# Attention, folded weights and two token-wise layers on one core: TensorE in the source's order through attention, sums of two pairs in four strips

## The chip, the cores and the metric

One NeuronCore of a Trainium2 chip runs the whole program in one launch. The metric is the device time of one execution in microseconds (us); the kernel before takes 824.54 us (median of 3 runs, 823.51 to 825.24). The engines are named as in the profile: PE (TensorE, with its weight loads PEld), ACT (ScalarE), DVE (VectorE), POOL (GpSimd), and SP, which only issues transfers.

## The reference

```
# q, k, v: [4, 12, 448, 64]; w1, w2: [768, 1024]; w3: [1024, 1024]; w_out: [1024, 768]
s = cap * tanh((q @ k.T) / sqrt(64) / cap)           # per batch and head, 448 x 448
attn = exp(s - max(s));  attn /= sum(attn) + 1e-9
x = (attn @ v), heads side by side                   # 1792 tokens x 768
h = ((x @ w1) * (x @ w2)) @ w3;  x = h @ w_out       # first layer
h = x @ w_in;  e = exp(h - max(h))                   # second layer
solu = h * (e / (sum(e) + 1e-9))
ln = (solu - mean) / sqrt(var + 1e-6) * g_ln
out = ln @ w_out2
```

Everything is float32. Weights come as 64-bit values in two 32-bit words.

## The kernel before, in words

**Three stretches.** From 0 to 431 us attention runs, and PE's gaps in it are filled with work that doesn't depend on it. From 431 to 581 us the rest of the first layer's products (`ab`, line 592) runs alone. From 581 us to the end the second layer runs; the change doesn't touch it.

**Attention.** The 48 heads are taken two at a time: 24 pairs, `n` = 0 to 23. A pair's 448 keys are four chunks, `c` = 0 to 3; chunks 0 to 2 hold 128 keys of each head, chunk 3 the last 64 keys of both. `scores(n, c, place_)` (line 226) multiplies keys by queries. For chunks 0 to 2 each head takes 64 rows of the array, so two matmuls (one for each head, line 238) stand in the two row halves; they come in three terms (high and low parts), six matmuls to a tile. Chunk 3 fills the whole array (line 234). A tile of scores lies in one of two places of PSUM, `sc0` and `sc1`, and a place can't be written again before ACT has taken tanh and exp of what is in it (`exps`, lines 246 and 247). `keep` (lines 255 to 261) lets DVE add up a pair's four exp tiles into one tile `s`, of which two buffers exist.

**The visit of the values.** `values(n)` (line 263) takes pair n's exp tiles to the output: first `n` (line 275), the sums over keys, by a matrix of ones 64 columns wide, once for each head; then `o` (lines 276 to 280), the exp tiles times v, four chunks for each of two heads. The heads take the two column halves of the array (64 columns each). These matmuls are plain float32; each leaves two records in the trace, so `n` leaves 4 and `o` 16. ACT copies both results out (lines 284, 285). `inverse` (line 290) gathers the sums of two pairs by two transfers of POOL's queue, takes reciprocals on DVE and stores them.

**Fill.** Beside attention stand: `f` of line 360 (the product of w3 and w_out, 576 matmuls of 256 columns), `f` of line 378 (times w_in, 288 of 512 columns), and the first 404 of the 1152 `ab` matmuls (line 592, 448 columns). `fill(ns)` (line 631) emits them from one list, a given nominal time at a call (109, 216 and 189 ns for one matmul). Their weights are loaded as 64-bit values, put together by three DVE instructions (lines 171 to 173) and split into a high part (ACT, line 177) and a low part (DVE, line 178). `ahead.step()` puts one such weight tile forward; it is called at each chunk that `phases` passes.

**Order.** `phases(g)` (line 665) emits two pairs in three phases: phase 0 has chunks (2g, 0) and (2g, 1), then (2g, 3); phase 1 has (2g, 2), (2g+1, 0), then (2g+1, 3); phase 2 has (2g+1, 1), (2g+1, 2). Phases 0 and 2 also hold a visit of the values, of the pair before. Fill of 6100 ns is emitted at the end of each phase from g = 1 on (line 694). But the order in which PE gets its instructions isn't that of the source: a scheduler at build time sorts them by priorities (`tc.high_priority`, lines 670 to 685) and by what a model of the machine holds for ready; `tc.issue_after` pins some of them behind others. What comes out is one fixed list for each engine. The order of DVE, ACT and the queues is the scheduler's too.

Of the kernel before, what the change touches and what calls it, by code (L numbers as in the profile page):

```python
# [9 lines left out]
F32 = mybir.dt.float32  # L10
# [3 lines left out]
ALU = mybir.AluOpType  # L14
# [4 lines left out]
P = 128  # L19
B, H, S, D = 4, 12, 448, 64  # L20
# [5 lines left out]
HALF = 512  # L26
SUMS = 112
# [2 lines left out]
THREE = ((0, 0), (0, 1), (1, 0))  # L30

NP, NCH = B * NPAIR, 4
FIRST = 4
NV = 2 * NCH
EXPS = 7
FILL = 6100
W3 = 9
WARM = 12
LANDS = 3
PASSES = ((0, 1), (2, 3))  # L40
SQ = 32
# [59 lines left out]
def attention_moe_solu(ctx: ExitStack, tc: tile.TileContext, q, k, v, cap, w12, w3t, wo, win, wout2, g_ln, out):  # L101
# [9 lines left out]
    pe, act, dve, pool, sync = nc.tensor, nc.scalar, nc.vector, nc.gpsimd, nc.sync  # L111
# [5 lines left out]
    r_dr = dram.tile([B, H, S], F32, name="r_dr")  # L117
# [6 lines left out]
    const = ctx.enter_context(tc.tile_pool(name="const", bufs=1))  # L124
    capt = const.tile([P, 1], F32, name="capt")
    qscale = const.tile([P, 1], F32, name="qscale")
    guard = const.tile([P, 1], F32, name="guard")
    neghalf = const.tile([P, 1], F32, name="neghalf")
    gt = const.tile([P, LINE // 4], F32, name="gt")[:, :NF]
    ones = const.tile([P, D], F32, name="ones")  # L130
    edge = ctx.enter_context(tc.tile_pool(name="edge", bufs=1, side="right"))
    edge.tile([P, (LINE - 32) // 4], F32, name="edge")
    conv = ctx.enter_context(tc.tile_pool(name="conv", bufs=1))
# [1 line left out]
    def opened(stack, name, side="left"):  # L135
        cm = tc.tile_pool(name=name, bufs=1, side=side, reuse_waits="tile")
        stack.append(cm)
        return cm.__enter__()

    def close(stack, to=0):  # L140
        while len(stack) > to:
            stack.pop().__exit__(None, None, None)

    right, left = [], []
    at = opened(right, "at", "right")
    ps_cm = tc.tile_pool(name="ps1", bufs=1, space=PSUM)
    ps = ps_cm.__enter__()
# [39 lines left out]
        ahead.add(key, lambda: landing(i, src.bitcast(U32), 2 * n, U32), lambda: convert(i, n), rest, gate, there)  # L187


    landed, ready, parts, outs, xr, stored, inv = {}, {}, {}, {}, {}, set(), [None]  # L190

    def load_pair(n):
        if n == 1:
# [26 lines left out]
    def take_values(n):  # L220
        if n < NP:
            ready[n] = *ready[n], landed.pop(n)

    tiled = [None]

    def scores(n, c, place_):

        qh, ql, kh, kl = ready[n][:4]
        sc = ps.tile([P, 2, HALF], F32, tag=f"sc{place_}", name=f"sc{n}_{c}")
        terms = ((kh, ql), (kl, qh), (kh, qh)) if n else ((kh, qh),)  # L230
        for m, (kk, qq) in enumerate(terms):
            keys = kk[:, c * P:(c + 1) * P]
            if c == 3:
                pe.matmul(sc[:, 0, :S], keys, qq, start=(m == 0), stop=(m == len(terms) - 1))
                continue
            for j in range(2):
                rows = slice(j * D, (j + 1) * D)
                tiled[0] = pe.matmul(sc[:, j, :S], keys[rows], qq[rows, :], start=(m == 0), stop=(m == len(terms) - 1))  # L238
        return sc

    exp_ = {}
# [1 line left out]
    def exps(n, c, sc):  # L243
        w = 2 if c < 3 else 1
        p = at.tile([P, w, S], F32, tag="p" if c < 3 else "pl", bufs=EXPS if c < 3 else 3, name=f"p{n}_{c}")
        act.activation(sc[:, :w, :S], sc[:, :w, :S], AF.Tanh, scale=qscale)  # L246
        exp_[n, c] = act.activation(p, sc[:, :w, :S], AF.Exp, scale=capt)  # L247
        return p

    def keep(n, c, p):  # L250

        parts[n, c] = p
        if c == 1:
            parts[n, "s"] = t = at.tile([P, 2, S], F32, tag="s", bufs=2, name=f"s{n}")
            dve.tensor_tensor(t, parts[n, 0], p, ALU.add)  # L255
            for j in range(2):
                rows = slice(j * D, (j + 1) * D)
                dve.tensor_tensor(t[rows, j], t[rows, j], parts[n, NCH - 1][rows, 0], ALU.add)
        elif c == 2:
            t = parts[n, "s"]  # L260
            dve.tensor_tensor(t, t, p, ALU.add)

    def values(n):

        b, m = divmod(n, NPAIR)
        vs = ready[n][4]
        out, total = (ps.tile([P, HALF], F32, tag="o", bufs=2, name=f"{x}{n}") for x in ("o", "n"))
        seen = [None]

        def product(dst, j, weights, moving, first, last):  # L270
            with tc.issue_after(seen[0].ins) if seen[0] is not None else nullcontext():
                seen[0] = pe.matmul(dst[j * D:(j + 1) * D, :S], weights, moving, start=first, stop=last)  # L272

        for j in range(2):
            product(total, j, ones, parts[n, "s"][:, j], True, True)
        for c in range(NCH - 1):
            for j in range(2):
                product(out, j, vs[:, j * (NCH - 1) + c], parts[n, c][:, j], c == 0, False)
        for j in range(2):
            product(out, j, vs[:, 2 * (NCH - 1) + j], parts[n, NCH - 1][:, 0], False, True)  # L280
        t = at.tile([P, S], F32, tag="x", bufs=2, name=f"x{n}")
        if m % 2 == 0:
            xr[b, m // 2] = at.tile([P, 2, S], F32, tag="xr", bufs=3, name=f"xr{b}_{m // 2}")
        act.copy(xr[b, m // 2][:, m % 2], out[:, :S])
        act.copy(t, total[:, :S])
        inverse(b, m, t)
        for c in (*range(NCH), "s"):
            del parts[n, c]

    def inverse(b, m, t):  # L290

        w = 4 * S // SUMS
        if m % 2 == 0:
            inv[0] = at.tile([SUMS, w], F32, tag="inv", bufs=2, name=f"inv{b}_{m}")
        r = inv[0]
        pool.dma_start(out=r[m % 2 * SUMS // 2:][:SUMS // 2], in_=t[::D])
        if m % 2 == 1:
            dve.tensor_scalar(r, r, guard[:SUMS], None, ALU.add)
            dve.reciprocal(r, r)
            pool.dma_start(out=r_dr[b, 2 * m - 2:2 * m + 2].rearrange("h s -> (h s)").rearrange("(p w) -> p w", p=SUMS), in_=r)  # L300
            stored.add((b, m // 2))


    fw, pos, place, held = {}, [0], {}, {}
# [326 lines left out]
    def fill(ns):  # L631
        owed[0] += ns
        while owed[0] > 0:
            d = next(work, None)
            if d is None:
                return False
            if d == 0:
                owed[0] = 0
            owed[0] -= d
        return True  # L640
# [4 lines left out]
    if WARM:  # L645

        zero = at.tile([P, 2, S], F32R, tag="p", bufs=EXPS, name="zero")
        dve.memset(raw(zero[:, 0]), 0.0)
        idle = ps.tile([P, HALF], F32, tag="f", bufs=2, name="idle")
# [15 lines left out]
    def phases(g):  # L665
        n, first = 2 * g, g % 2
        for phase in range(3):
            run = (((n, 0), (n, 1)), ((n, 2), (n + 1, 0)), ((n + 1, 1), (n + 1, 2)))[phase]
            one, two = (first, 1 - first) if phase != 1 else (1 - first, first)
            with tc.high_priority():  # L670
                tiles = [scores(*run[0], one)]
                with tc.issue_after(tiled[0].ins):
                    tiles.append(scores(*run[1], two))
            if not g and not phase:
                with tc.issue_after(tiled[0].ins):
                    for i in range(WARM // 2):
                        pe.matmul(idle[:, :S], zero[:, 0, :P], zero[:, 0], start=True, stop=True)
            if phase != 1 and n + phase:
                with tc.issue_after(tiled[0].ins), tc.high_priority(offset=400):
                    values(n - 1 + phase // 2)  # L680
            for turn, x in enumerate((run[0], (n + phase, 3), run[1])):
                if turn == 1:
                    if phase == 2:
                        continue
                    with tc.high_priority():
                        sc = scores(*x, one)
                else:
                    sc = tiles[turn // 2]
                keep(*x, exps(*x, sc))
                if g or phase:  # L690
                    with tc.issue_after(exp_[0, 1].ins) if not g else nullcontext():
                        ahead.step(2 if g >= NP // 4 else 1)
            if g:
                fill(FILL)
            if phase != 1 and 0 < n + phase // 2 < NP - 1:
                m = n + 1 + phase // 2
                split_pair(m)
                take_values(m)
                if m + 1 < NP:
                    with tc.issue_after(loads[max(loads)].ins) if g < 2 else nullcontext():  # L700
                        load_pair(m + 1)
            if not g and phase == 1:
                with tc.issue_after(loads[max(loads)].ins):
                    load_pair(2)

    for g in range(NP // 2):
        phases(g)
    values(NP - 1)
    close(right)
    wsp = opened(right, "ws", "right")  # L710
    place["ws"] = ws = {m: wsp.tile([P, 2, NF // 2, HALF], F32R, tag=f"w{m}", name=f"ws{m}") for m in EARLY[:4]}
# [14 lines left out]
    ps = ps_cm.__enter__()  # L726
    PAIRS = NT // P // 2
    LAST = PAIRS - 1
    wg, banks, keeps, h, a, x, sums, es, sts = {}, {}, {}, {}, {0: begun}, {0: (lands.pop("x0"), lands.pop("x1"))}, {0: {}}, {}, {}
# [324 lines left out]
```

## Time and profile before

| | |
|---|---|
| median of 3 runs | 824.54 us (823.51 to 825.24) |
| the profiled execution | 824.29 us, of which the span from first to last instruction 822.5 us |
| busy: PE, DVE, ACT, POOL | 800.3, 564.5, 442.6, 55.8 us |
| mean granted clock of PE | 0.988 |

The profile page shows shares of the whole span. The stretch that the change touches, 0 to 431 us, is read from windows and from the timeline. In a timeline row the time is that of the first start, and the second number reaches from there to the end of the last record; matmuls overlap, so the pace of a run is read from start to start. "Idle before <- X" names what the engine waited for.

### The profile page before, as it was taken

The page shows a single profiled execution, that of the slowest core. Times are in us where ns is not written, and L with a number is a line of the kernel's source. Part 1 is how long each engine was busy: PE and PEld are TensorE (multiplying, and loading weights), DVE is VectorE, ACT ScalarE, POOL GpSimd, SP SyncE. Part 2 cuts the span into 40 slices and gives each one's busy share as a digit, 9 for nine tenths or more (in the row PEclk, how much of TensorE's full clock was granted, in tenths as well). Part 3 has the DMA queues.
Part 4 walks back from the last instruction along what each step waited for, and adds up shares of the span by engine and source line. Part 5 has one row for each costly group of instructions (what it writes and reads, how often), then busy time and mean ns, then how long its engine had stood idle before and what let it go on. Part 6 is the DMA issues. An engine that isn't in the chain of part 4 may idle for free.

```text
span 822.5 us, 11645 instructions
## 1 busy us (share of the span) xinstructions
PE 800.3 (97%) x4187; PEld 639.9 (78%) x4187; DVE 564.5 (69%) x1006; ACT 442.6 (54%) x654; POOL 55.8 (7%) x106
## 2 busy tenths in 40 slices
PE   6898999999999999999999999999999999999998
PEld 4566867865755676766779999999878888899997
DVE  6999886688675467668666554432496678888972
ACT  6684567666676666567623221111466667844642
POOL 0010000010010010110000100000011111100000
PEclk8899999999999999999999999999999999999999
DMA  5676963667784636367577599992724335996531
GB/s 201 227 209 196 307 209 115 177 188 275 237 281 147 198 94 205 95 246 263 194 223 239 155 365 403 355 332 84 208 61 154 102 110 122 249 237 127 142 91 77
DMA packets 145801, 162.47 MB, mean 198 GB/s; under 512 B 66720, under 2 KB 116432, under 8 KB 144208
## 3 DMA queue, kind: packets, MB, share of 16 engines
q1 hardware_dynamic: 143056, 156.01, 59.5%
q0 software_dynamic: 2688, 5.72, 3.0%
q8 instruction: 33, 0.54, 0.3%
q14 instruction: 24, 0.20, 0.1%
HBM read 114.04 MB, written 47.53 MB: 196 GB/s over the span
## 4 chain that ended last, share of the span: by engine, by line
PE 74%; DVE 11%; DMA 10%; issue 3%; ACT 1%; SPq 0%; POOL 0%; DVEq 0%; POOLq 0%
PE ab L592 26%; PE u L741 15%; PE v L741 8%; PE f L378 6%; PE o L272 6%; PE y L741 4%; PE sc L238 4%; PE f L360 3%; DVE cv L173 2%; DMA qd<-in_q 2%; DVE cv L172 2%; PE n L272 2%; DMA inv<-x 1%; DMA ld<-in_win 1%; DMA wg<-wg_dr 1%
## 5 line engine op out<-in xcount | busy, mean ns | idle before, releaser
L592 PE MATMUL ab<-xs,wt 128*128 128x448 f32 x1152 | 238.3, 364 | 0.0
L592 PEld LDWEIGHTS ab<-xs,wt 128*128 128x128 f32 x1152 | 214.2, 188 | 26.2 <-issue 10.4
L246 ACT ACTIVATE sc<-sc,qscale 128x896 f32<-128x896 f32 (+1 forms) x96 | 84.8, 885 | 42.9 <-PE sc L238 29.8
L247 ACT ACTIVATE p<-sc,capt 128x896 f32<-128x896 f32 (+1 forms) x96 | 87.9, 918 | 1.8
L360 PEld LDWEIGHTS f<-w,w_o 128*128 128x128 f32 x576 | 73.2, 195 | 17.5 <-issue 10.6
L360 PE MATMUL f<-w,w_o 128*128 128x256 f32 x576 | 80.3, 292 | 4.6 <-ACT w L177 1.6
L272 PE MATMUL o<-p,vd 128*64 128x448 f32 x384 | 80.7, 541 | 0.0
L741 PE MATMUL u<-ws,a 128*128 128x512 f32 x336 | 80.2, 390 | 0.3 <-DVE a L869 0.3
L378 PE MATMUL f<-w_i,w 128*128 128x512 f32 x288 | 73.1, 402 | 1.6 <-ACT w L177 1.3
L741 PEld LDWEIGHTS u<-ws,a 128*128 128x128 f32 x336 | 63.0, 188 | 13.9 <-DVE a L869 0.7
L378 PEld LDWEIGHTS f<-w_i,w 128*128 128x128 f32 x288 | 53.1, 190 | 21.6 <-issue 8.4
L272 PEld LDWEIGHTS o<-p,vd 128*64 128x64 f32 x384 | 27.9, 138 | 45.6 <-issue 44.1
L741 PE MATMUL u<-wg,a 128*128 128x384 f32 x336 | 62.0, 334 | 0.0
L596 ACT COPY a<-ab 128x448 f32<-128x448 f32 x32 | 17.0, 532 | 81.4 <-PE ab L592 67.7
L600 DVE TENSOR_TENSOR abs<-ab,a 128x448 f32<-128x448 f32 x32 | 19.9, 622 | 58.2 <-PE ab L592 48.0
L741 PEld LDWEIGHTS u<-wg,a 128*128 128x128 f32 x336 | 58.5, 188 | 0.3 <-DVE a L869 0.2
L172 DVE SCALAR_TENSOR_TENSOR cv<-ld,cv 128x512 uint32<-128x512 uint32 (+1 forms) x80 | 52.0, 660 | 0.8
L173 DVE SCALAR_TENSOR_TENSOR cv<-ld,cv 128x512 uint32<-128x512 uint32 (+1 forms) x80 | 52.0, 660 | 0.8
L171 DVE TENSOR_SCALAR cv<-ld 128x512 uint32<-128x512 uint32 (+1 forms) x80 | 32.4, 412 | 25.3 <-DMA ld<-in_w 14.6
L865 ACT CAST a<-s 128x512 fp32r<-128x512 f32 (+1 forms) x42 | 31.3, 754 | 31.2 <-DVE s L887 17.0
L255 DVE TENSOR_TENSOR s<-p,p 128x896 f32<-128x896 f32 x24 | 26.1, 1087 | 22.1 <-ACT p L247 22.1
L741 PE MATMUL v<-ws,a 128*128 128x512 f32 x168 | 40.4, 389 | 0.0
(132 smaller groups left out, 1111.5 us busy)
## 6 DMA issues: line engine op xcount, KB each, us to landing
ld<-in_w SPq DMA_DIRECT2D x24, 512.0 KB, 4.8
w_dr<-wt SPq DMA_DIRECT2D x6, 1536.0 KB, 6.9
wt<-w_dr SPq DMA_DIRECT2D x6, 1536.0 KB, 8.9
ld<-in_w3t SPq DMA_DIRECT2D x16, 512.0 KB, 4.6
ab_dr<-abs SPq DMA_DIRECT2D x32, 224.0 KB, 3.7
ldx<-ab_dr SPq DMA_DIRECT2D x14, 512.0 KB, 4.5
c_dr<-h SPq DMA_DIRECT2D x14, 512.0 KB, 2.6
ldx<-c_dr SPq DMA_DIRECT2D x56, 128.0 KB, 3.2
```

The lines of the kernel that those rows point to most:

```text
L171: dve.tensor_scalar(x, hi, 5, 2, ALU.logical_shift_left, ALU.logical_shift_right)
L172: dve.scalar_tensor_tensor(x, hi, 0xC0000000, x, ALU.bitwise_and, ALU.bitwise_or)
L173: dve.scalar_tensor_tensor(x, lo, 29, x, ALU.logical_shift_right, ALU.bitwise_or)
L238: tiled[0] = pe.matmul(sc[:, j, :S], keys[rows], qq[rows, :], start=(m == 0), stop=(m == len(terms) - 1))
L246: act.activation(sc[:, :w, :S], sc[:, :w, :S], AF.Tanh, scale=qscale)
L247: exp_[n, c] = act.activation(p, sc[:, :w, :S], AF.Exp, scale=capt)
L272: seen[0] = pe.matmul(dst[j * D:(j + 1) * D, :S], weights, moving, start=first, stop=last)
L360: pe.matmul(f[:, :QW], lw[:, a], rw[:, e], start=(g == 0 and m == 0), stop=(g == NF - 1 and m == 2))
L378: pe.matmul(f, w34[:, a, c, :], rw[:, e], start=(c == 0 and m == 0), stop=(c == NC - 1 and m == 2))
L592: pe.matmul(pp[f, b, i][:, :S], w[:, u], xs[b, c][:, e], start=(c == 0 and m == 0), stop=(c == NC - 1 and m == 2))
L741: pe.matmul(banks[g], a[r][m][:, p, k * P:(k + 1) * P], b[m][:, e, k, :], start=(first and k == 0 and i == 0), stop=(k == NF // 2 - 1 and ...
L865: act.copy(both[r, m][0], source(r, m))
```

## The change

1. The visits of the sums are taken once for two pairs, at the odd pair: `ones` is `SQ` = 32 columns wide, and four matmuls (two pairs, two heads) go to four 32-column strips of one PSUM tile. A pair's `s` is kept until then. ACT copies the sums once for two pairs, POOL gathers them by one transfer instead of two. The sums now stand behind `o` in the visit. There are five `xr` buffers instead of three.
2. PE's order in attention is the source's (`manual_schedule` for PE alone); all `issue_after` and `high_priority` around it are gone. The two score tiles of a phase stand back to back, the visit of the values right behind them.
3. Fill is emitted in two halves, one ahead of the phase's chunk 3 and one at its end, by a table: nominally 0, 0, 1300 ns in the three phases of g = 0; 2000, 3000, 3000; 4000, 5000, 5000; 6000, 6500, 6500; 7000, 7000, 7000 for g = 1 to 4; and 5000, 9000, 5600 from g = 5 on.

```diff
-    ones = const.tile([P, D], F32, name="ones")
+    ones = const.tile([P, SQ], F32, name="ones")
...
+FILLS = ((0, 0, 1300), (2000, 3000, 3000), (4000, 5000, 5000), (6000, 6500, 6500), (7000, 7000, 7000))
+LATER = (5000, 9000, 5600)
...
-        out, total = (ps.tile([P, HALF], F32, tag="o", bufs=2, name=f"{x}{n}") for x in ("o", "n"))
...
-        for j in range(2):
-            product(total, j, ones, parts[n, "s"][:, j], True, True)
+        out = ps.tile([P, HALF], F32, tag="o", bufs=2, name=f"o{n}")
         for c in range(NCH - 1):
             for j in range(2):
-                product(out, j, vs[:, j * (NCH - 1) + c], parts[n, c][:, j], c == 0, False)
+                pe.matmul(out[j * D:(j + 1) * D, :S], vs[:, j * (NCH - 1) + c], parts[n, c][:, j], start=(c == 0), stop=False)
...
         act.copy(xr[b, m // 2][:, m % 2], out[:, :S])
-        act.copy(t, total[:, :S])
-        inverse(b, m, t)
+        if m % 2 == 1:
+            total = ps.tile([P, HALF], F32, tag="o", bufs=2, name=f"n{n}")
+            for i in range(4):
+                pe.matmul(total[i * SQ:(i + 1) * SQ, :S], ones, parts[n - 1 + i // 2, "s"][:, i % 2], start=True, stop=True)
+            t = at.tile([P, S], F32, tag="x", bufs=2, name=f"x{n}")
+            act.copy(t, total[:, :S])
+            inverse(b, m, t)
...
-            with tc.high_priority():
-                tiles = [scores(*run[0], one)]
-                with tc.issue_after(tiled[0].ins):
-                    tiles.append(scores(*run[1], two))
+            filling = (FILLS[g] if g < len(FILLS) else LATER)[phase] / 2
+            tiles = [scores(*run[0], one), scores(*run[1], two)]
...
             for turn, x in enumerate((run[0], (n + phase, 3), run[1])):
                 if turn == 1:
+                    fill(filling)
...
-            if g:
-                fill(FILL)
+            fill(filling)
...
-    for g in range(NP // 2):
-        phases(g)
-    values(NP - 1)
+    with tc.manual_schedule(engines={pe.engine}):
+        for g in range(NP // 2):
+            phases(g)
+        values(NP - 1)
```

On PE, behind the third score tile of pair 4, stood in the kernel before (the number behind `sc`, `o`, `n`, `s`, `p` is the pair, the one behind it the chunk; `f1` is the fill of line 360, `w_3` and `w_o` its weights):

```order
L238 MATMUL sc4_2_958<-ql4_783,kh4_786 128x448 x2
L238 MATMUL sc4_2_958<-qh4_782,kl4_787 128x448 x2
L238 MATMUL sc4_2_958<-qh4_782,kh4_786 128x448 x2
L360 MATMUL f1_0_4_587<-w_3_0_2_347,w_o_4_1_608 128x256 x6
L360 MATMUL f1_0_4_587<-w_3_0_3_363,w_o_4_1_608 128x256 x6
L360 MATMUL f1_0_5_692<-w_3_0_0_275,w_o_4_1_608 128x256 x6
L360 MATMUL f1_0_5_692<-w_3_0_1_288,w_o_4_1_608 128x256 x6
L360 MATMUL f1_0_5_692<-w_3_0_2_347,w_o_4_1_608 128x256 x6
L360 MATMUL f1_0_5_692<-w_3_0_3_363,w_o_4_1_608 128x256 x6
L360 MATMUL f1_1_0_721<-w_3_1_0_722,w_o_0_0_210 128x256 x6
```

and there stands now:

```order
L237 MATMUL sc4_2_768<-ql4_616,kh4_619 128x448 x2
L237 MATMUL sc4_2_768<-qh4_615,kl4_620 128x448 x2
L237 MATMUL sc4_2_768<-qh4_615,kh4_619 128x448 x2
L237 MATMUL sc5_0_775<-ql5_755,kh5_758 128x448 x2
L237 MATMUL sc5_0_775<-qh5_754,kl5_759 128x448 x2
L237 MATMUL sc5_0_775<-qh5_754,kh5_758 128x448 x2
L353 MATMUL f1_0_5_750<-w_3_0_0_270,w_o_4_1_668 128x256 x3
L353 MATMUL f1_0_5_750<-w_3_0_1_290,w_o_4_1_668 128x256 x6
L353 MATMUL f1_0_5_750<-w_3_0_2_358,w_o_4_1_668 128x256 x6
L353 MATMUL f1_0_5_750<-w_3_0_3_373,w_o_4_1_668 128x256 x6
L353 MATMUL f1_1_0_820<-w_3_1_0_786,w_o_0_0_212 128x256
L233 MATMUL sc5_3_822<-ql5_755,kh5_758 128x448
```

What moved: pair 5's first tile follows pair 4's last, and 22 matmuls of fill stand behind it ahead of pair 5's chunk 3. Before, 142 matmuls of fill stood between these two tiles.

Around the sums of pair 15 PE's list was:

```order
L238 MATMUL sc16_1_2910<-ql16_2890,kh16_2893 128x448 x2
L238 MATMUL sc16_1_2910<-qh16_2889,kl16_2894 128x448 x2
L238 MATMUL sc16_1_2910<-qh16_2889,kh16_2893 128x448 x2
L272 MATMUL n15_2918<-s15_2839,ones_74 64x448 x2
L592 MATMUL ab0_0_0_2871<-xs0_0_2224,wt0_2130 128x448
L592 MATMUL ab0_0_0_2871<-xs0_1_2225,wt0_2130 128x448 x3
L592 MATMUL ab0_0_0_2871<-xs0_2_2424,wt0_2130 128x448 x3
L592 MATMUL ab0_0_0_2871<-xs0_3_2425,wt0_2130 128x448 x3
L592 MATMUL ab0_0_0_2871<-xs0_4_2434,wt0_2130 128x448 x3
L592 MATMUL ab0_0_0_2871<-xs0_5_2435,wt0_2130 128x448 x3
L592 MATMUL ab1_0_0_2984<-xs0_0_2224,wt0_2130 128x448 x3
L592 MATMUL ab1_0_0_2984<-xs0_1_2225,wt0_2130 128x448
```

and is now:

```order
L237 MATMUL sc16_1_2835<-ql16_2815,kh16_2818 128x448 x2
L237 MATMUL sc16_1_2835<-qh16_2814,kl16_2819 128x448 x2
L237 MATMUL sc16_1_2835<-qh16_2814,kh16_2818 128x448 x2
L269 MATMUL o15_2842<-p15_0_2706,vd15_2534 64x448 x2
L269 MATMUL o15_2842<-p15_1_2764,vd15_2534 64x448 x2
L269 MATMUL o15_2842<-p15_2_2793,vd15_2534 64x448 x2
L271 MATMUL o15_2842<-p15_3_2703,vd15_2534 64x448 x2
L278 MATMUL n15_2852<-s14_2613,ones_74 32x448 x2
L278 MATMUL n15_2852<-s15_2767,ones_74 32x448 x2
L371 MATMUL f2_7_1_2808<-w_i_0_0_1923,w34_7_1_2779 128x512 x4
L371 MATMUL f2_7_1_2808<-w_i_1_1_2041,w34_7_1_2779 128x512 x8
L233 MATMUL sc16_3_2879<-ql16_2815,kh16_2818 128x448
```

What moved: `n15` stood alone between score tiles and fill, with `o15` 24 matmuls of fill and chunk 3 behind it, and in two pieces. Now `o15` and the sums of pairs 14 and 15 follow the two score tiles in one piece, and chunk 3 stands between two halves of the fill.

## Rows read from the trace of the kernel before

**Rows 1.** The page, parts 1 and 4: busy time, and the chain by engine.
```profile
PE 800.3 (97%) x4187; PEld 639.9 (78%) x4187; DVE 564.5 (69%) x1006; ACT 442.6 (54%) x654; POOL 55.8 (7%) x106
...
PE 74%; DVE 11%; DMA 10%; issue 3%; ACT 1%; SPq 0%; POOL 0%; DVEq 0%; POOLq 0%
```
**Rows 2.** Windows by stage: busy of PE, PEld, DVE, ACT, POOL; PEclk, DMA share, GB/s.
```profile
0.00:73.70 73.70, 63.52 (x352) 41.77 (x352) 63.60 (x115) 50.59 (x73) 5.55 (x14) 0.91 0.66 210
73.70:112.60 38.90, 34.45 (x247) 28.84 (x246) 34.49 (x64) 20.11 (x33) 0.86 (x1) 0.96 0.80 258
...
105.00:160.00 55.00, 53.39 (x363) 38.62 (x362) 39.10 (x67) 37.35 (x55) 3.61 (x6) 1.00 0.55 169
...
205.00:290.00 85.00, 85.00 (x419) 55.94 (x418) 50.26 (x80) 55.67 (x80) 9.13 (x18) 1.00 0.66 211
...
350.00:431.00 81.00, 80.52 (x405) 56.38 (x403) 58.96 (x110) 45.53 (x67) 6.32 (x10) 1.00 0.67 230
431.00:581.00 150.00, 150.00 (x751) 140.55 (x751) 67.21 (x133) 30.82 (x49) 2.72 (x7) 1.00 0.77 267
```
**Rows 3.** Timeline of PE, 43 to 58 us: start, length, instructions.
```profile
43.89 0.47 PE L238 MATMUL sc<-ql,kh 64*128 64x448 f32 x2
...
44.70 1.44 PE L360 MATMUL f<-w,w_o 128*128 128x256 f32 x10
...
50.99 0.97 PE L272 MATMUL n<-s,ones 128*64 128x448 f32 x4
51.79 3.18 PE L272 MATMUL o<-p,vd 128*64 128x448 f32 x16
54.90 1.70 PE L360 MATMUL f<-w,w_o 128*128 128x256 f32 x12
56.52 0.47 PE L238 MATMUL sc<-ql,kh 64*128 64x448 f32 x2
...
57.93 1.93 PE L360 MATMUL f<-w,w_o 128*128 128x256 f32 x14
```
**Rows 4.** Timeline of PE in two narrow windows, inside one visit of the values.
```profile
50.99 0.60 PE L272 MATMUL n<-s,ones 128*64 128x448 f32 x2
...
51.41 0.55 PE L272 MATMUL n<-s,ones 128*64 128x448 f32 x2
51.79 0.55 PE L272 MATMUL o<-p,vd 128*64 128x448 f32 x2
```
**Rows 5.** Timeline of DVE: the last add of pair 4's sums.
```profile
72.65 1.08 DVE L261 TENSOR_TENSOR s<-s,p 128x896 f32<-128x896 f32 x1
```
**Rows 6.** Timeline of PE: the end of pair 7's visit.
```profile
146.32 0.96 PE L272 MATMUL o<-p,vd 128*64 128x448 f32 x2
147.21 0.73 PE L360 MATMUL f<-w,w_o 128*128 128x256 f32 x4
```
**Rows 7.** Waits of PE, 20 to 431 us: in total, times, longest.
```profile
PE n L272 <- DVE s L261: 2.1, 2, 1.6
PE f L360 <- ACT w L177: 1.6, 1, 1.6
PE f L378 <- ACT w L177: 1.3, 1, 1.3
```
**Rows 8.** Groups of instructions of ACT, by form: tanh and exp.
```profile
L247 ACT ACTIVATE p<-sc,capt 128x896 f32<-128x896 f32 x72 | 72.8, 1012 | 1.2
L246 ACT ACTIVATE sc<-sc,qscale 128x896 f32<-128x896 f32 x72 | 70.2, 977 | 29.8 <-PE sc L238 29.8
...
L247 ACT ACTIVATE p<-sc,capt 128x448 f32<-128x448 f32 x24 | 15.2, 634 | 0.6
...
L246 ACT ACTIVATE sc<-sc,qscale 128x448 f32<-128x448 f32 x24 | 14.6, 610 | 13.1 <-PE sc L234 13.0
```

More of the change, by code (lines that the diff above doesn't have):

```diff
@@ L32 @@
 NP, NCH = B * NPAIR, 4
-FIRST = 4
 NV = 2 * NCH
 EXPS = 7
-FILL = 6100
+FILLS = ((0, 0, 1300), (2000, 3000, 3000), (4000, 5000, 5000), (6000, 6500, 6500), (7000, 7000, 7000))
+LATER = (5000, 9000, 5600)
 W3 = 9
@@ L187, in plan64 @@
         ahead.add(key, lambda: landing(i, src.bitcast(U32), 2 * n, U32), lambda: convert(i, n), rest, gate, there)
-    landed, ready, parts, outs, xr, stored, inv = {}, {}, {}, {}, {}, set(), [None]
+    landed, ready, parts, xr, stored = {}, {}, {}, {}, set()
     def load_pair(n):
@@ L222, in take_values @@
             ready[n] = *ready[n], landed.pop(n)
-    tiled = [None]
     def scores(n, c, place_):
@@ L237, in scores @@
                 rows = slice(j * D, (j + 1) * D)
-                tiled[0] = pe.matmul(sc[:, j, :S], keys[rows], qq[rows, :], start=(m == 0), stop=(m == len(terms) - 1))
+                pe.matmul(sc[:, j, :S], keys[rows], qq[rows, :], start=(m == 0), stop=(m == len(terms) - 1))
         return sc
@@ L266, in values @@
         vs = ready[n][4]
-        out, total = (ps.tile([P, HALF], F32, tag="o", bufs=2, name=f"{x}{n}") for x in ("o", "n"))
[L268 to L272, printed above, removed]
-        for j in range(2):
-            product(total, j, ones, parts[n, "s"][:, j], True, True)
+        out = ps.tile([P, HALF], F32, tag="o", bufs=2, name=f"o{n}")
@@ L276, in values @@
         for c in range(NCH - 1):
             for j in range(2):
-                product(out, j, vs[:, j * (NCH - 1) + c], parts[n, c][:, j], c == 0, False)
+                pe.matmul(out[j * D:(j + 1) * D, :S], vs[:, j * (NCH - 1) + c], parts[n, c][:, j], start=(c == 0), stop=False)
         for j in range(2):
-            product(out, j, vs[:, 2 * (NCH - 1) + j], parts[n, NCH - 1][:, 0], False, True)
-        t = at.tile([P, S], F32, tag="x", bufs=2, name=f"x{n}")
+            pe.matmul(out[j * D:(j + 1) * D, :S], vs[:, 2 * (NCH - 1) + j], parts[n, NCH - 1][:, 0], start=False, stop=True)
@@ L282, in values @@
         if m % 2 == 0:
-            xr[b, m // 2] = at.tile([P, 2, S], F32, tag="xr", bufs=3, name=f"xr{b}_{m // 2}")
+            xr[b, m // 2] = at.tile([P, 2, S], F32, tag="xr", bufs=5, name=f"xr{b}_{m // 2}")
         act.copy(xr[b, m // 2][:, m % 2], out[:, :S])
-        act.copy(t, total[:, :S])
-        inverse(b, m, t)
-        for c in (*range(NCH), "s"):
+        if m % 2 == 1:
[5 more added lines that the diff above has]
+            inverse(b, m, t)
+            for i in range(2):
+                del parts[n - i, "s"]
@@ L288, in values @@
+        for c in range(NCH):
             del parts[n, c]
     def inverse(b, m, t):
[L292 to L301, printed above, removed]
+        r = at.tile([SUMS, 4 * S // SUMS], F32, tag="inv", bufs=2, name=f"inv{b}_{m}")
@@ L304, in attention_moe_solu @@
+        pool.dma_start(out=r, in_=t[::SQ])
+        dve.tensor_scalar(r, r, guard[:SUMS], None, ALU.add)
+        dve.reciprocal(r, r)
+        pool.dma_start(out=r_dr[b, 2 * m - 2:2 * m + 2].rearrange("h s -> (h s)").rearrange("(p w) -> p w", p=SUMS), in_=r)
+        stored.add((b, m // 2))
     fw, pos, place, held = {}, [0], {}, {}
@@ L669, in phases @@
             one, two = (first, 1 - first) if phase != 1 else (1 - first, first)
-            with tc.high_priority():
-                tiles = [scores(*run[0], one)]
-                with tc.issue_after(tiled[0].ins):
-                    tiles.append(scores(*run[1], two))
+            filling = (FILLS[g] if g < len(FILLS) else LATER)[phase] / 2
+            tiles = [scores(*run[0], one), scores(*run[1], two)]
             if not g and not phase:
-                with tc.issue_after(tiled[0].ins):
-                    for i in range(WARM // 2):
-                        pe.matmul(idle[:, :S], zero[:, 0, :P], zero[:, 0], start=True, stop=True)
+                for i in range(WARM // 2):
+                    pe.matmul(idle[:, :S], zero[:, 0, :P], zero[:, 0], start=True, stop=True)
             if phase != 1 and n + phase:
-                with tc.issue_after(tiled[0].ins), tc.high_priority(offset=400):
-                    values(n - 1 + phase // 2)
+                values(n - 1 + phase // 2)
             for turn, x in enumerate((run[0], (n + phase, 3), run[1])):
                 if turn == 1:
+                    fill(filling)
                     if phase == 2:
                         continue
-                    with tc.high_priority():
-                        sc = scores(*x, one)
+                    sc = scores(*x, one)
                 else:
```

## The prediction

> **What bounds the kernel now.** I read the page's busy times and chain first, then windows by stage, then PE's timeline around a visit of the values, then DVE's timeline and the waits. PE is busy 97% of the span, and 74% of the chain that ended last lies on it [rows 1]. So a gain must come from PE's own work or from the few places where PE starves. The windows show these places [rows 2]: from 0 to 73.7 us PE is busy 63.52, from 73.7 to 112.6 us 34.45 of 38.90, while from 205 to 290 us and from 431 to 581 us nothing is left. The early stretch is short of weights and exp tiles: DVE is busy 63.60 of 73.70 us in 115 instructions (0.553 us each), then 34.49 of 38.90 in 64 (0.539 each, 0.608 with its waits). The waits that end PE's idle time agree: the longest are for pair 5's sums from DVE and for weights from ACT [rows 7].
>
> **Prices of PE's work.** In a run of fill an `f` matmul of 256 columns costs (1.62 - 0.10) / 12 = 0.127 us, from the start at 54.90 to the next at 56.52 with one change of shape taken off [rows 3]. A change of shape (row halves, column halves, full array) costs about 0.10: three pairs of score matmuls between fill took 0.81 (43.89 to 44.70), six in one run 1.41 (56.52 to 57.93), so a pair is 0.20 and entering and leaving is about 0.2 for two changes [rows 3]. `n` takes 0.80 (50.99 to 51.79), of which I put 0.75 to the four passes, and `o` about 3.1 (51.79 to 54.90) [rows 3]. An `ab` matmul is 150.00 / 751 = 0.200 [rows 2].
>
> **Part 1, sums in four strips.** Each matmul leaves two records, one for each pass. Two records start as one pair at 50.99, the next two at 51.41, and `o` follows at 51.79 [rows 4]: the two column halves run beside each other. A sum thus takes 0.75 for two heads. If four strips run beside each other as two halves do, four heads take that 0.75 as well. From below: nothing gives less than one visit's 0.75, since each strip still has all its columns to pass. From above: two and two, 1.50. I take 0.75, since the halves show full overlap. From pair 8 on there are 16 sums before and 8 after: 16 x 0.75 - 8 x 0.75 = 6.0 us. These lie on the path, as PE has next to no idle time there. Twelve of ACT's copies of the sums and twelve transfers of POOL's queue go; ACT and POOL are busy 54% and 7% [rows 1], so I cost that at nothing. DVE's first add of a pair's `s` gets a new wait, as `s` has two buffers and both are held until the odd pair's visit: the add of pair 2g waits for the sums of pairs 2g-2 and 2g-1. These stand right behind the two score tiles of the same phase, and the exps that the add needs take two times 1.99 us [rows 8], longer than the rest of the visit. So it waits under 1 us, and behind it on DVE stand weights for later fill. With that cover gone, 12 x 1 us on DVE, which is busy 50.26 of 85 us in the windows from 205 us [rows 2].
>
> **Part 2, the source's order.** PE's list has 162 changes of shape before and 97 after. Up to the end of pair 7's visit they are 55 and 33, so 107 and 64 behind it; the sums in four strips add 8 switches of column width there, which I price alike, so 72. That is 35 x 0.10 = 3.5 us. Bounds: a change between row halves and full array may be cheaper than the 0.10 from [rows 3] (0.05, gain 1.8) or dearer (0.15, gain 5.3).
>
> **Part 3, the table of fill, and the early stretch.** Here I compare the end of pair 7's visit, 147.21 us before [rows 6], at equal work. After, 389 `f` matmuls are done by then instead of 450: 61 x 0.127 = 7.7 us less. Before also had one score tile and one chunk 3 more, 1.2 us. So the time before at equal work is 147.2 - 7.7 - 1.2 = 138.3.
>
> For the time after I start from DVE, which sets the pace. The last add of pair 4's sums ends at 72.65 + 1.08 = 73.7 [rows 5]; by then DVE has done 114 of its instructions. In the new order 118 stand up to the same add: 73.7 x 118 / 114 = about 76. From there to the weight tile that the fill ahead of pair 5's second tile needs (`w_3_1_3`) are 17 instructions, 17 x 0.608 = 10.3, so 86. Then PE has 6 `f` (0.76), six pairs of scores (1.41), `o4` (3.1), 46 `f` (5.84), six pairs again (1.41) and `o5` (3.1): 15.6, so the sums of pairs 4 and 5 start at about 101. DVE alone allows it: 41 instructions to pair 5's last add are 41 x 0.608 = 25, from 76 to 101. With DVE dense (0.539) it would be 98 by DVE and 100.5 by PE; I keep 101.
>
> From there to the end of pair 7's visit PE has 175 `f` (22.2), six tiles of scores (3.6) and two chunks 3 (1.2), two visits of `o` (6.0), the sums of pairs 4 and 5 and of 6 and 7 (1.5), and nine or ten changes (0.95): 35.45, which ends at 136.5. The gain is 138.3 - 136.5 = 1.8 us. It is small because the fewer sums and changes there are partly used up by PE starving: the list holds less fill early (214 `f` ahead of `o5`, 349 before), so what DVE delays isn't covered. Bounds: with DVE dense 2.3, with DVE's waits doubled 0.
>
> Behind attention 4 more `ab` are left, 4 x 0.200 = 0.8 us lost. The transfers of the early stretch (DMA share 0.80 [rows 2]) carry the same bytes.
>
> **The sum.** 1.8 + 6.0 + 3.5 - 0.8 = 10.5 us. The profiled execution took 824.29 us with a span of 822.5, so 1.8 us lie around it; it is 0.25 below the median. 822.5 - 10.5 + 1.8 = 813.8. This holds PE's other waits, 1.3 us for weights from ACT among them [rows 7], and its granted clock (1.00 from 105 us on but for stretches [rows 2]) as they were.
>
> **Rivals.** *The strips don't run four at a time.* For it: the trace shows no four strips, only halves. Two and two, each sum visit takes 1.50 instead of 0.75. Ten such visits stand from pair 5's on, so 7.5 us go back: 813.8 + 7.5 = 821.3. Half of it (1.13 a visit) would give 817.6. Against it: two halves overlap wholly [rows 4]. On this the Trainium skill speaks, in TensorE: Matmul & The Clock Gate, Part 3, "The mechanism": matmuls start and end strictly in the order of the program. By that rule a plain float32 matmul's second pass would hold up the next strip, and four strips would overlap only at their edges. The halves of [rows 4] start together all the same, so here the trace speaks against it so far.
>
> *Slower: PE waits in the source's order for ACT.* PE can no longer pass a chunk 3 or a run whose place ACT hasn't emptied. A place is free after tanh and exp, 0.98 + 1.01 us for a tile and 0.61 + 0.63 for a chunk 3 [rows 8], and ACT has casts and copies of fill in the same queue, which themselves wait for PE. From pair 5's visit on there are 27 phases; the gain of 10.5 is gone at 0.4 us a phase. If in the 18 phases with a chunk 3 its 1.24 us lie bare, 22.3 us are lost: 813.8 + 22.3 = 836. For it: before, tanh waits 29.8 us in all for scores [rows 8], so it runs close behind PE. Against it: by the prices above half a phase's fill (2.5 to 4.5 us nominal) stands between a tile and the next use of its place, and ACT is busy 55.67 of 85 [rows 2].
>
> *The early stretch is paced by the loads of weights, not by DVE's count.* Before, 11 weight tiles were begun between 73.7 and 112.6, 3.54 us each, at a DMA share of 0.80 [rows 2]. After, nine stand up to pair 5's last add: 76 + 9 x 3.54 = 107.9, 6.9 later: 820.7. Against it: DVE's waits there are only 4.4 of 38.9 us.
>
> *Better: the other idle time goes as well.* If the list follows what DVE and ACT deliver, half of the 10.2 + 4.5 = 14.6 us of idle time up to 112.6 [rows 2] could go: 813.8 - 7.3 = 806.5.
>
> **How the numbers follow.** Forecast, 809 to 818: 0.50. Strips not four at a time: 0.17. Slower by ACT: 0.14. Loads: 0.10. Better: 0.09. The range 804 to 823 leaves out the slower case and the ends of the others. About 0.2% (1.65 us) is what a measurement of this kernel can tell from no change. Faster takes the forecast, the better case, nearly all of the loads and most of the strips: 0.78. Same takes the upper ends of strips and loads: 0.07. Slower 0.15.
>
> **What would show it.** The strips: the timeline inside a sums' visit has four starts together (or two, 0.4 us apart and 1.5 us in all), and PE's busy time falls by 6 to 9 us from sums and changes together. The order: score runs of six pairs take 1.41 everywhere. The early part: pair 5's sums start near 101 us and pair 7's visit ends near 136. The ACT rival: waits of PE's score matmuls for ACT's exp in the phases from 140 us on, over 10 us in all. The prediction is wrong if PE's idle time from 140 to 431 us grows beyond 3 us, or if pair 7's visit ends after 140.

## The result: slower by 0.6%, and the profile after

The changed kernel takes 829.5 us (median of 8 runs, 826.53 to 832.79) against 824.64 (8 runs) in the same jobs: ratio 1.0062, 95% interval 1.004 to 1.0084. Forecast were 813.8 us and a gain. The profiled execution took 832.79 us (span 831.0), 8.5 more than the one before; it is the slowest of the eight, and the medians lie 4.9 apart.

The page, part 1, answers to [rows 1]:

```profile
PE 792.8 (95%) x4187; PEld 640.5 (77%) x4187; DVE 564.7 (68%) x1006; ACT 435.9 (52%) x642; POOL 48.8 (6%) x94
```

PE is busy 7.5 us less, inside the 6 to 9 that sums and changes of shape were to give; but busy time also holds what a lower clock and a slower second layer added, so it doesn't confirm these prices (the table at the end of the experiments takes it apart). The span is 8.5 longer: 16 us more of PE's time stand empty. The windows by stage (columns as in [rows 2]) show where:

```profile
0.00:73.70 73.70, 61.87 (x343) 39.26 (x344) 62.92 (x115) 50.51 (x71) 4.30 (x12) 0.91 0.67 226
73.70:112.60 38.90, 34.62 (x202) 25.18 (x203) 32.44 (x57) 18.82 (x30) 1.24 (x2) 0.78 0.70 207
105.00:160.00 55.00, 54.88 (x421) 46.40 (x423) 34.98 (x61) 31.85 (x51) 2.46 (x4) 1.00 0.52 155
160.00:205.00 45.00, 41.03 (x232) 28.69 (x229) 36.21 (x61) 29.48 (x44) 4.01 (x8) 1.00 0.72 207
205.00:290.00 85.00, 77.34 (x372) 51.37 (x372) 51.70 (x81) 51.01 (x73) 5.81 (x10) 0.96 0.66 213
...
350.00:431.00 81.00, 79.16 (x429) 58.72 (x429) 66.06 (x121) 50.06 (x73) 3.76 (x6) 1.00 0.67 231
```

From 205 to 290 us PE was full in [rows 2]; now 7.7 us are missing there, and the granted clock fell to 0.96. From 73.7 to 112.6 us the busy time is the same, but at 0.78 instead of 0.96. Within it:

```profile
70.00:75.00 5.00, 2.49 (x19) 2.08 (x17) 4.32 (x11) 3.72 (x6) 0.56 (x1) 0.99 0.71 213
75.00:80.00 5.00, 3.39 (x10) 2.44 (x10) 4.97 (x9) 2.21 (x5) 0.00 (x0) 0.50 0.76 229
...
85.00:90.00 5.00, 4.44 (x19) 3.25 (x21) 4.93 (x9) 2.72 (x5) 0.00 (x0) 0.50 0.82 243
```

The clock falls to its lower level, 1.2 GHz, behind 5 us in which PE was half empty. DVE is full from 75 us on (4.97 of 5 us), and PE's waits from 65 to 105 us, 6.5 in all, are all for weights. What PE waits for from 147 to 300 us, then from 300 to 440 us, answers to [rows 7] (total us, times, longest):

```profile
PE f L371 <- DVE w L179: 9.8, 5, 3.5
PE f L371 <- ACT w L178: 1.9, 2, 1.4
...
PE ab L585 <- DVE abs L593: 4.2, 2, 2.4
```

So the longest new wait is for the weights of the fill of line 371 (line 378 before). The visits of the sums come later than forecast, but take the time forecast. PE's timeline at the sums of pairs 4 and 5 and at the end of pair 7's visit (answers to [rows 3, 6]):

```profile
104.03 0.96 PE L278 MATMUL n<-s,ones 128*32 128x448 f32 x8
104.92 3.62 PE L353 MATMUL f<-w,w_o 128*128 128x256 f32 x28
...
138.04 0.96 PE L278 MATMUL n<-s,ones 128*32 128x448 f32 x8
138.93 4.10 PE L353 MATMUL f<-w,w_o 128*128 128x256 f32 x32
```

Four strips with eight records take 0.89 us with their change of shape: they run beside each other. Last, the second layer, where no line is changed, takes 246.0 us instead of 241.8 (from the first `u` to the end). PE's timeline there, two rows of before and two of after:

```profile
644.14 2.88 PE L741 MATMUL u<-ws,a 128*128 128x512 f32 x12
646.87 2.88 PE L741 MATMUL v<-ws,a 128*128 128x512 f32 x12
```
```profile
646.46 2.96 PE L730 MATMUL y<-ws,a 128*128 128x512 f32 x12
649.26 2.96 PE L730 MATMUL u<-ws,a 128*128 128x512 f32 x12
```

From one group's start to the next, twelve matmuls take 2.72 to 2.73 us in most groups of before and 2.80 in most of after, both at a granted clock of 1.00.

### The profile page after: what moved, and what is told of

The parts are those of the page before. It is cut to its first block, busy times and chain, and to the rows that moved or that the text cites. A ratio compares the mean times of both kernels' runs of the same rounds, so it can differ in the third digit from the quotient of the medians.

```text
span 831.0 us, 11560 instructions
## 1 busy us (share of the span) xinstructions
PE 792.8 (95%) x4187; PEld 640.5 (77%) x4187; DVE 564.7 (68%) x1006; ACT 435.9 (52%) x642; POOL 48.8 (6%) x94
## 4 chain that ended last, share of the span: by engine, by line
PE 55%; DVE 9%; DMA 9%; issue 3%; ACT 2%; POOL 0%; DVEq 0%; POOLq 0%; ACTq 0%
PE ab L585 21%; PE u L730 15%; PE v L730 8%; PE y L730 4%; PE f L371 3%; DMA ld<-in_w 3%; PE o L269 2%; DMA rb<-r_dr 2%; PE sc L237 1%; DMA wg<-wg_dr 1%; DVE w L179 1%; DMA wg_dr<-wg 1%; DVE cv L173 1%; DVE xr L446 1%; DVE cv L174 1%
## 5 line engine op out<-in xcount | busy, mean ns | idle before, releaser
L353 PE MATMUL f<-w,w_o 128*128 128x256 f32 x576 | 78.4, 291 | 7.3 <-DVE w_o L179 2.9
L371 PE MATMUL f<-w_i,w 128*128 128x512 f32 x288 | 72.6, 400 | 11.6 <-DVE w L179 9.8
L730 PEld LDWEIGHTS u<-ws,a 128*128 128x128 f32 x336 | 63.0, 188 | 15.1 <-DVE a L858 0.7
L269 PE MATMUL o<-p,vd 128*64 128x448 f32 x288 | 64.6, 587 | 0.0
L254 DVE TENSOR_TENSOR s<-p,p 128x896 f32<-128x896 f32 x24 | 26.1, 1088 | 31.4 <-PE n L278 31.2
L269 PEld LDWEIGHTS o<-p,vd 128*64 128x64 f32 x288 | 20.0, 148 | 34.1 <-issue 33.6
```

Source lines behind the costliest of these rows:

```text
L269: pe.matmul(out[j * D:(j + 1) * D, :S], vs[:, j * (NCH - 1) + c], parts[n, c][:, j], start=(c == 0), stop=False)
L353: pe.matmul(f[:, :QW], lw[:, a], rw[:, e], start=(g == 0 and m == 0), stop=(g == NF - 1 and m == 2))
L371: pe.matmul(f, w34[:, a, c, :], rw[:, e], start=(c == 0 and m == 0), stop=(c == NC - 1 and m == 2))
L730: pe.matmul(banks[g], a[r][m][:, p, k * P:(k + 1) * P], b[m][:, e, k, :], start=(first and k == 0 and i == 0), stop=(k == NF // 2 - 1 and ...
```

## The experiments

Unless said otherwise they are edits of the changed kernel. Each was timed beside the kernel before on its chip; ratios are to that.

**Parts alone.** Theories: the fixed order and its table lost the time; or the sums of two pairs did, through DVE's wait for them.

e1_strips_only, an edit of the kernel before:

```diff
-    ones = const.tile([P, D], F32, name="ones")
+    ones = const.tile([P, SQ], F32, name="ones")
...
+        if m % 2 == 1:
+            for i in range(4):
+                product(total, i, ones, parts[n - 1 + i // 2, "s"][:, i % 2], True, True, SQ)
```

> The kernel before with part 1 alone: one visit of the sums for two pairs in four strips (and five xr buffers), the scheduler's order of TensorE and the flat 6100 ns of fill kept. Theory A (the order and the table of fill lost it, the strips give what was priced): the strips save 12 x 0.75 us less what lay in early idle time, 6 to 8 us: 817 to 819 us beside 824.6. Theory B (the sums of two pairs themselves cost it, because DVE's first add of the next even pair waits for them): 824 us or more, with waits of s for n on DVE of over 25 us.

822.76 us, ratio 0.9969 (0.995 to 0.9988): faster, so in the scheduler's order the sums of two pairs don't cost the time, but the gain is 2.6 us where 6 to 8 were expected. e10 finds the rest.

e2_flat_fill:

```diff
-            filling = (FILLS[g] if g < len(FILLS) else LATER)[phase] / 2
+            filling = 3050 if g else 0
```

> The changed kernel with the table of fill undone: 3050 + 3050 ns in every phase from g = 1 on, as much as before, still in two halves and in the source's order. If the table asks for more fill between 160 and 300 us than weights are ready for (table theory): PE's waits there for weights fall from 11.7 to under 4 us and the time to 819 to 822 us. If it is the fixed order itself, in which PE stands still at the first weight tile that is late whatever the table (order theory): 827 to 832 us, with at least 8 us of such waits.

828.77 us (822.9 to 830.97), ratio 1.0029 (1.0004 to 1.0055). The profiled execution is its fastest, 822.9 us, so it shows less waiting than a usual one may have. Its idle time from 160 to 300 us is 5.3 instead of 11.6, but from 20 to 105 us 15.1 instead of 10.5: the flat table is better late and worse early. It settles neither theory.

e3_pair_sums:

```diff
-        if m % 2 == 1:
+        total = ps.tile([P, HALF], F32, tag="o", bufs=2, name=f"n{n}")
+        for j in range(2):
+            pe.matmul(total[j * D:(j + 1) * D, :S], ones, parts[n, "s"][:, j], start=True, stop=True)
```

> The changed kernel with part 1 undone: sums of each pair at its own visit, two strips of 64 columns, behind o; source order and table kept. If PE's own work sets the time: 12 more sums of about 0.8 us and a change of shape each, some of it beside waits: 835 to 840 us. If PE waits for weights in the stretch anyway (its pace is that of the supply), the added work falls into the waits: 829 to 832 us.

831.71 us, ratio 1.0068 (1.0039 to 1.0097): as the second reading had it. But the edit also brings back the wide tile of ones, which makes another part faster (e6, below). Against e6, which has that tile as well, the added sums cost 0.47%, 3.9 us (the two intervals overlap slightly); only the rest of their work falls into the waits. And without any sum of two pairs PE still waits 9.4 us for the same weights:

```profile
PE f L373 <- DVE w L179: 7.5, 5, 3.0
PE f L373 <- ACT w L178: 1.9, 2, 1.6
```

That is a second blow to the theory of DVE's wait for the sums.

e5_no_manual:

```diff
-    with tc.manual_schedule(engines={pe.engine}):
+    if True:
```

> The changed kernel with only the fixed order of TensorE taken away: the scheduler orders PE again, without the old priorities and pins; strips and table kept. PE's list has 206 changes of shape instead of 97, 109 x 0.10 = 11 us more work. Order theory: PE no longer stands at late weights between 160 and 300 us, waits there under 4 us: -10 + 11, 828 to 832 us with PE busy near 803. Table theory: the waits stay, 836 to 841 us.

822.98 us, ratio 0.9978 (0.996 to 0.9996), 5 us better than the low end expected. With the same table PE is never idle in this stretch:

```profile
160.00:300.00 140.00, 140.00 (x669) 87.61 (x667) 93.73 (x150) 88.48 (x128) 11.70 (x24) 1.00 0.64 205
```

PE is busy 808.6 us, 15.8 more than after. So it takes both: the table, and the fixed order. A PE that is merely slower, and so gives the weights time, isn't the reason: by 240 us it has begun 177 of the 288 matmuls of this fill, the changed kernel 158. That other work passes a late weight tile here is the likely reading; no run tries it alone.

**The second layer.** In these profiles a pace of 2.80 us for twelve matmuls went with the narrow tile of ones, also in the scheduler's order. All of SBUF that is allocated behind it lies 128 bytes nearer.

e6_after_padded:

```diff
-    ones = const.tile([P, SQ], F32, name="ones")
+    ones = const.tile([P, D], F32, name="ones")[:, :SQ]
```

> The changed kernel with the tile of ones allocated 64 columns wide as before and 32 of them used, so that all that is allocated behind it lies where it lay before, 128 bytes further. Layout theory (the second layer's matmuls, in which no line is changed, run at 0.2333 and 0.1758 us in the profiles of the three kernels with the narrow tile and at 0.2267 and 0.1733 in the two with the wide one, because of where their operands lie): 0.2267 and 0.1733 here, the second layer 241.8 to 244 us instead of 246.0, and 825 to 827 us instead of 829.5. Chance theory (this pace differs from run to run or chip to chip): no relation to the tile's width, 828 to 831 us.

827.24 us, ratio 1.0021 (1.0 to 1.0042).

e7_before_shifted, an edit of the kernel before:

```diff
     ones = const.tile([P, D], F32, name="ones")
+    const.tile([P, SQ], F32, name="shift")
```

> The kernel before with one unused tile of 128 bytes behind the ones, nothing else changed. Layout theory: the second layer's paces go to 0.2333 and 0.1758 and the time to 827 to 829 us if 128 bytes either way are as bad; chance theory: 824 to 826 us and paces without relation to it.

828.05 us, ratio 1.0024 (1.0008 to 1.004), 2.0 us slower by the ratio. PE's timeline in the second layer, of e6 and then of e7:

```profile
648.07 2.88 PE L730 MATMUL u<-ws,a 128*128 128x512 f32 x12
650.79 2.88 PE L730 MATMUL v<-ws,a 128*128 128x512 f32 x12
```
```profile
646.45 2.96 PE L742 MATMUL u<-ws,a 128*128 128x512 f32 x12
649.25 2.96 PE L742 MATMUL v<-ws,a 128*128 128x512 f32 x12
```

The place alone sets it, in either kernel: in most groups 2.72 or 2.80 us, and a second layer of 242 us in e6 and 245 in e7. It went so in the profiles of sixteen kernels, eleven with the old places and five with shifted ones.

e10_strips_padded, e1 with the edit of e6:

> The kernel before with the four strips alone, the scheduler's order, and the wide tile of ones. Layout theory: 2.5 to 4.5 us faster than with the narrow tile (822.8), so 818 to 820 us, with the second layer at 0.2267 and 0.1733 us. Chance theory: 821.5 to 824 us.

818.39 us, ratio 0.991 (0.9884 to 0.9935). In the scheduler's order the strips are worth 7.4 us.

**The table.** The next five have the wide tile of ones. e8, e15 and e16 stand against e6, e11 and e13 against e8.

e8_less_fill:

```diff
-FILLS = ((0, 0, 1300), (2000, 3000, 3000), (4000, 5000, 5000), (6000, 6500, 6500), (7000, 7000, 7000))
-LATER = (5000, 9000, 5600)
+FILLS = ((0, 0, 1300), (2000, 3000, 3000), (4000, 5000, 5000), (6000, 6500, 6500))
+LATER = (5000, 6500, 5000)
```

> The changed kernel with the wide tile of ones and a table that asks for less fill from g = 4 on: 5000, 6500, 5000 ns instead of 7000, 7000, 7000 and 5000, 9000, 5600. Supply theory (PE stands still between 160 and 300 us because the table runs ahead of the weights; the fill left over does as well behind attention, where PE never waits): waits for weights there fall from 11.7 us to under 4, 6 to 8 us less than e6. Order theory (a late weight tile stops PE wherever it stands): waits stay over 8 us, time within 3 us of e6.

813.59 us, ratio 0.9857 (0.9835 to 0.988): 13.6 less than e6. The waits for weights from 160 to 300 us (e6, then e8):

```profile
PE f L371 <- DVE w L179: 7.8, 4, 3.1
PE f L371 <- ACT w L178: 2.3, 1, 2.3
```
```profile
PE f L371 <- DVE w L179: 3.0, 1, 3.0
```

e15_later_only changes only `LATER`, e16_g4_only only the entry of g = 4 (the first two lines, then the last two):

```diff
-LATER = (5000, 9000, 5600)
+LATER = (5000, 6500, 5000)
...
-FILLS = ((0, 0, 1300), (2000, 3000, 3000), (4000, 5000, 5000), (6000, 6500, 6500), (7000, 7000, 7000))
+FILLS = ((0, 0, 1300), (2000, 3000, 3000), (4000, 5000, 5000), (6000, 6500, 6500), (5000, 6500, 5000))
```

> e6_after_padded (827.2 us) with only the table's last entry changed, 5000, 6500, 5000 ns from g = 5 on instead of 5000, 9000, 5600; g = 4 keeps 7000. If the 9000 is what runs ahead of the weights: nearly all of e8's gain, 813 to 817 us. If it is the 7000 of g = 4, whose debt is carried on: 822 to 826 us.

> e6_after_padded with only the entry of g = 4 changed, 5000, 6500, 5000 instead of 7000, 7000, 7000; from g = 5 on 5000, 9000, 5600 stay. If the 9000 does it: 824 to 827 us; if g = 4: 815 to 819 us.

e15: 824.76 us, ratio 0.9987 (0.9968 to 1.0007); e16: 814.11 us, ratio 0.9871 (0.9849 to 0.9893). By the ratios, e15 gains 2.8 us on e6 and e16 12.4. I had guessed the 9000; it is g = 4. Where `f` of line 371 begins in after, and its longest waits (two windows of PE's timeline), then where it begins in e16, and e16's waits from 160 to 300 us:

```profile
169.18 0.86 PE L371 MATMUL f<-w_i,w 128*128 128x512 f32 x3
...
189.42 2.34 PE L371 MATMUL f<-w_i,w 128*128 128x512 f32 x9 [3.47 <-DVE w L179]
...
211.57 1.22 PE L371 MATMUL f<-w_i,w 128*128 128x512 f32 x2 [2.60 <-DVE w L179]
```
```profile
174.56 1.33 PE L371 MATMUL f<-w_i,w 128*128 128x512 f32 x5
```
```profile
PE n L278 <- DVE s L260: 1.3, 1, 1.3
PE f L371 <- ACT w L178: 1.3, 1, 1.3
PE f L371 <- DVE w L179: 0.7, 2, 0.4
```

7000 ns a phase in g = 4 use up the fill of line 353 early, so that of line 371 begins 5.4 us sooner, before its weights are in stock. In the source, weights are put forward a fixed number of times for each chunk (once up to g = 5, twice from g = 6 on), so a phase with more fill gets no more of them.

e11_least_fill lowers e8's table further from g = 7 on, and e13_early_table moves fill from g = 1 to g = 2 (the first four lines, then the last two; both as edits of e8):

```diff
-FILLS = ((0, 0, 1300), (2000, 3000, 3000), (4000, 5000, 5000), (6000, 6500, 6500))
-LATER = (5000, 6500, 5000)
+FILLS = ((0, 0, 1300), (2000, 3000, 3000), (4000, 5000, 5000), (6000, 6500, 6500), (5000,6500,5000), (5000,6500,5000), (5000,6500,5000))
+LATER = (4500, 5500, 4500)
...
-FILLS = ((0, 0, 1300), (2000, 3000, 3000), (4000, 5000, 5000), (6000, 6500, 6500))
+FILLS = ((0, 0, 1300), (2000, 2500, 2500), (4500, 5500, 5500), (6000, 6500, 6500))
```

> As e8_less_fill with still less fill from g = 7 on: 4500, 5500, 4500 ns. Supply theory: in e8 PE no longer waits for weights behind 300 us, so less there gives nothing: 812.5 to 814.5 us, the waits between 160 and 300 us as in e8 (4.1 us). If PE would rather wait for ACT once fill gets scarce (ACT theory): 816 us or more, with waits of scores for exp.

> e8_less_fill with the fill of g = 1 moved to g = 2 (2000, 2500, 2500 and 4500, 5500, 5500 ns): the same table theory for the 9 us of idle time between 20 and 105 us. If the table runs ahead of the weights there too: idle time there 6 to 8 us and 811 to 813 us. If these waits are for DVE's pace whatever stands in the list: 813 to 815 us.

e11: 815.16 us, ratio 0.9885 (0.9865 to 0.9904), not different from e8 by these intervals. e13: 814.15 us (810.26 to 820.55), ratio 0.9878 (0.9838 to 0.9918): no gain shown; its idle time from 20 to 105 us is 12.5, not 6 to 8, in its fastest execution (e8: 9.3). DVE is busy 79.7 of these 85 us; that its pace sets the early waits fits, but isn't shown.

**Strips and order where the supply isn't short.** e12_less_fill_pair_sums is e8 with the edit of e3, e14_less_fill_no_manual e8 with that of e5, e17_early_pair e12 with e13's table.

> e8_less_fill with part 1 undone: sums of each pair at its own visit, two strips of 64 columns, source order. Where PE hardly waits, the price of the strips shows whole: 12 sums of 0.8 us and their changes of shape more, 8 to 11 us: 821.5 to 824.5 us. If what PE does beside its waits is hidden even here: under 818 us.

> e8_less_fill without the fixed order of TensorE: the price of the order once the supply is not short. Some 100 changes of shape more at 0.10 us against waits of 4 us that go: 6 us slower, 818 to 821 us. If the order gives nothing: 812 to 815 us.

> e12_less_fill_pair_sums (each pair's own sums, 813.3 us) with the early table of e13. If the strips' work is only moved into waits for weights: equal to e13, 812 to 815 us. If pairs' sums cost what they should once the early table is better too: 817 to 820 us.

e14: 825.33 us, ratio 1.0004 (0.999 to 1.0018), by the ratios 12 us slower than e8. It has 211 changes of shape to e8's 97, and 114 x 0.10 = 11.4; but this agreement is chance. By the table below, e14 has 34.1 us more of work, 10.8 less idle time and loses 12.0 less by the clock. The work is not only changes of shape: the pins that kept a visit together are gone, and here one half of an `o` product stands alone among score tiles:

```profile
123.07 0.97 PE L269 MATMUL o<-p,vd 128*64 128x448 f32 x2
123.96 0.48 PE L237 MATMUL sc<-ql,kh 64*128 64x448 f32 x2
```

Its two records take 0.89 us to the next start, as long as the eight of a sums' visit in four strips. 52 of the 384 records of `o` stand alone in e14, none in e8.

e12: 813.31 us, ratio 0.9862 (0.9844 to 0.9881), against my expectation no slower than e8. e17: 817.17 us, ratio 0.9896 (0.987 to 0.9922); its median is what the second reading expected, but e13's ratio lies inside that interval, so the two readings aren't told apart. The windows of e8, then of e12:

```profile
160.00:200.00 40.00, 37.01 (x215) 26.34 (x213) 34.11 (x57) 26.80 (x41) 3.84 (x8) 0.95 0.73 214
200.00:250.00 50.00, 48.94 (x246) 32.00 (x243) 36.13 (x59) 37.19 (x54) 5.18 (x10) 0.97 0.72 234
```
```profile
160.00:200.00 40.00, 37.35 (x224) 26.96 (x224) 33.95 (x57) 27.16 (x43) 5.12 (x10) 1.00 0.71 209
200.00:250.00 50.00, 49.54 (x245) 33.40 (x242) 37.14 (x60) 39.81 (x59) 5.80 (x11) 1.00 0.78 260
```

Each span can be split by windows of 5 us into PE's idle time, what the clock lost (busy time x (1 - granted clock)), and the rest, PE's work at full clock:

| us | idle | lost by the clock | rest | span |
|---|---|---|---|---|
| before | 22.2 | 8.5 | 791.9 | 822.5 |
| after | 38.2 | 15.0 | 777.8 | 831.0 |
| e3, pairs' sums | 35.3 | 13.3 | 781.4 | 830.0 |
| e6, wide tile | 38.0 | 15.2 | 773.4 | 826.6 |
| e8, less fill | 26.9 | 14.6 | 770.9 | 812.4 |
| e12, e8 with pairs' sums | 25.5 | 8.1 | 778.1 | 811.7 |
| e14, e8 without the order | 16.1 | 2.6 | 805.0 | 823.6 |

The strips take 7 to 8 us of work off PE in the source's order too (e3 to e6, e12 to e8). In e8 they come back, as 1.4 us of idle time and 6.5 of clock. This isn't one execution's doing: the mean granted clock was 0.977 to 0.983 in all five runs of e8 and 0.987 to 0.991 in all four of e12. Whether the lighter work made it fall is open.

## Why the prediction was wrong

In the profiled executions attention was to end at 431.0 - 1.8 - 6.0 - 3.5 = 419.7 us and ended at 434.1, 14.4 later; the second layer added 4.3, the stretch of `ab` 0.3: together the 19.0 us between forecast (-10.5) and measurement (+8.5). In the table's terms PE's work at full clock fell by 14.1 us, although the second layer grew; 16.0 us more idle time and 6.5 more lost by the clock ate that up.

- *The step that failed* is the last sentence of the sum: "This holds PE's other waits ... and its granted clock ... as they were". From the end of pair 7's visit to the end of attention PE waited 15.9 us against 2.1 before, a sign of being wrong that the prediction had named. I priced part 3 only up to pair 7 and took the later entries of the table for harmless, though they were in the diff. e8 shows 13.6 us for the table, e16 that the entry of g = 4 alone gives 12.4 by the ratios, e5 that the same table costs no waits from 160 to 300 us where the scheduler may move fill. My slower rival had the right kind, PE standing still in the source's order, but the wrong place: ACT's places of scores instead of weights. Its sign of 10 us of waits for exp didn't come.
- *Early stretch:* the sums of pairs 4 and 5 began at 104.0 instead of 101, pair 7's visit ended at 138.9 instead of 136.5: a gain of -0.6 instead of 1.8. Part of it is a slip: 76 + 10.3 + 15.6 makes 101.9, not 101. The idle time behind it was in the sum; the clock at half speed from 75 us on wasn't.
- *The strips:* right in mechanism (0.89 us with a change of shape; the rival falls), worth 7.4 us in the scheduler's order (e10). In the source's order 3.9 us (e3 to e6, 0.47%), and no difference shows in e12 against e8: 7.2 us less work came back as clock and idle time. I had called the path PE's behind pair 8.
- *Changes of shape:* the price of 0.10 us each wasn't tested alone. Against before, with the same sums, e12 has 65 changes fewer and 13.8 us less work, 0.21 each; but there too more went than changes, as 24 records of `o` stood alone in before and none in e12. The source's order was worth more than the 3.5 us of the sum, through visits in one piece as well.
- *DVE's new wait for the sums,* put at under 1 us each and costed at nothing: DVE waits 31.2 us for them in six places, where the same add waited 22.1 us for exp before; e3 shows that this isn't what starves PE.
- *Not seen at all:* the narrower tile of ones moved everything behind it by 128 bytes and made the untouched second layer 4 us longer; 3.4 us of the result (e6). That e8 comes out at 813.6, close to the 813.8, is chance: the early gain and the strips' are missing there, and the order is worth more than I gave it.

## What to carry to other kernels

A fixed order of the busiest engine takes away its freedom to pass a late operand, so the amount of filler in each stretch must be held against the rate of its supply, stretch by stretch; here 21 of 864 fill matmuls more by pair 10's visit (644 instead of 623) cost some 12 us. Price such a table along its whole length, not up to where the last idle time stood before. And when a small constant tile changes size, pad it: it moves the operands of code that nobody touched. Both kernels are beaten by the source's order with a smaller table and a padded tile: 813.3 to 814.1 us (e8, e12, e16).

## What the runs showed of the hardware

The pace of the second layer's matmuls of 512 columns, 12 in 2.72 or in 2.80 us at the same granted clock of 1.00, hangs here on where SBUF operands lie, by 128 bytes (e6, e7); which operand it is wasn't tried. And idle time of PE can be paid twice: in after it was half empty from 70 to 75 us, and from 75 to 90 us its granted clock was 0.50, 1.2 GHz; over the whole span 38.2 us of idle time came with 15.0 lost by the clock, in the kernel before 22.2 with 8.5. It is no fixed price: in e8 26.9 us of idle time came with 14.6 lost, in e12 25.5 with 8.1.
